# Moving padded chunk data as two transfers of 48 rows instead of one of 104, in a recurrence followed by two feed-forward layers

## The chip, the cores and the metric

The kernel runs on one core of a Trainium2 chip. The metric is the device time of one execution in microseconds (us), lower being better; the figure of a kernel is the median of its runs.

## The reference

Three stages follow one another. The first is a recurrence over 768 steps for 4 batches of 8 heads, each head with a state of 40 x 40; the second and third are feed-forward layers over the 3072 resulting tokens, with 320 inputs, 2048 hidden units and 320 outputs, all in float32.

```python
for t in range(S):                                # S = 768, state [B, H, 40, 40]
    y[:, :, t] = np.einsum('bhd,bhde->bhe', rt, state)
    Sa = np.einsum('bhde,bhe->bhd', state, at)
    state_decay = state * wt[:, :, None, :] - np.einsum('bhd,bhe->bhde', Sa, bt)
    state = state_decay + np.einsum('bhd,bhe->bhde', vt, kt)
...
h = x @ w_in;  g = h * (1.0 / (1.0 + np.exp(-1.702 * h)));  x = g @ w_out      # layer 1
h = x @ w_in;  g = h - np.tanh(h);                          x = g @ w_out      # layer 2
```

## The kernel before

The recurrence is cut into 24 chunks of 32 steps. For each chunk the products that do not need the state are formed first, then a small triangular system is inverted for a group of chunks, and then the state passes through the chunk.

The 32 heads (4 batches times 8) lie on the partitions as two halves, one at partitions 0 to 39 and one at 64 to 103, because each head has 40 channels and a half starts at a multiple of 64. The host pads each half to 64 rows, so one chunk is stored as 128 rows, of which rows 40 to 63 and 104 to 127 are padding. Moving rows 0 to 103 in one transfer takes both halves and the padding between them.

The methods that matter here:

- `early(c)` loads a chunk of `pin` into the buffer `P` (two buffers, used in turn). A row of `P` is 2065 floats: the decays at `OW`, then `a` at `OA`, then `k` and `b` from `OF` to `PC`. VectorE forms running products of the decays (L391, L397, L399), VectorE or GpSimd multiply them into the other parts (L394, L400, L402), TensorE forms the chunk's products (L416, L441). From chunk 2 on, the finished `P` is written to DRAM (`spill`), and small results go there too (`ka`, `ui`). `early` also loads `rve` (r and v) and `vns`.
- `inverse` and `inverse_halves` invert the triangular systems of a group of chunks, on GpSimd, step by step (L472, L475).
- `late(c)` brings the chunk's pieces back from `spill`, `ka` and `ui` in other layouts (`FW`, `L1`, `U`). `receptance(c)` loads `R`, and `decay(c)` reads `W` back from `spill`.
- `chain(c, g)` passes the state through chunk `c` (lines 608 to 683), and `store(c)` writes the result to DRAM.
- `layer1(j)` and `layer2(n)` are the two feed-forward layers (matrix products at L777). The seven blocks of `layer1` can start as soon as the chunks they need are stored, so they are interleaved with the recurrence.

All transfers are issued by SyncE through the helper `dma` (L367), so every issue has that line and is told apart by its tiles. SyncE takes them in the order in which they were put; an issue whose condition is not met holds up those behind it.

The order is static. Each `Plan.add` records a task with its engine, a planned cost, its reads and writes, and a rank. `Plan.run` then plays the tasks through a list scheduler (lowest rank first among those that are ready) and emits the instructions in that order, for each engine. A task with `alt` may be given to either of two engines. The ranks come from the constants at the top of the file (`ERANK`, `TRANK`, `L1RANK`, `LEAD`, `LATE` and others).

In the kernel before, a load of a chunk from chunk 2 on is one transfer:

```python
rows = 128 if c < 2 else 104
if c < 2:
    spans = [(OW, OA, [kw]), (OF, PC, kf), (OA, OF, [ka])]
else:
    spans = [(OW, PC, [kw, ka] + kf)]
```

Of the kernel before, what the change touches and what calls it, by code (L numbers as in the profile page):

```python
# [49 lines left out]
DENSE = 1.4  # L50
LEAD = 2.8824
OLAG = 1.5654
OLAG2 = 5.0633
PLAG = 1.9246
KLAG = -0.79715
W1RANK = -3.0783
W1STEP = 0.34953
W2RANK = 26.554
W2STEP = 0.79772
BUSY = -5  # L60
LATE = 2.3095
LATEK = 17.86
G1 = -0.86755
G2 = 0.47713
WI = 0.66347
WO = 0.31035
ERANK = [-10.488, -9.3866, -2.6101, -1.8742, -0.68695, 0.36407, 0.75062, 1.827, 2.2989, 3.1149, 4.0456, 5.1374, 6.4967,
         7.2956, 8.2655, 9.2836, 10.145, 11.291, 11.988, 12.804, 11.168, 15.748, 15.401, 16.869]
TRANK = [-10.117, 1.5844, 2.2273, 5.6823, 12.206, 5.8527, 13.273]
L1RANK = [2.1663, 6.6107, 7.7041, 11.297, 16.428, 24.217, 27.763]  # L70
L1STEP = [0.17239, 0.19469, 0.27164, 0.27454, 0.31295, 0.23795, 0.27849]
# [48 lines left out]

class Task:
# [3 lines left out]
class Plan:  # L125
# [6 lines left out]
    def add(self, eng, cost, fn, r=(), w=(), rank=0.0, bank=None, of=None, alt=None, size=0, after=(), warm=False):  # L132


        t = Task()
        t.eng, t.cost, t.fn, t.rank, t.bank, t.of, t.alt, t.size, t.warm = eng, cost, fn, rank, bank, of, alt, size, warm
        t.n, t.out, t.users, t.tile, t.started, t.soon = len(self.tasks), [], 0, None, False, 0.0
        deps = set(after)
        if of is not None:
            deps.add(of)  # L140
            of.users += 1

        t.after = {self.last[k] for k in (*r, *w) if k in self.last}
# [12 lines left out]
        t.left = len(deps)  # L156
        for d in deps:
            d.out.append(t)
        self.tasks.append(t)
        return t  # L160

    def run(self, free):
# [14 lines left out]
        while events and done < len(self.tasks):  # L177
# [19 lines left out]
            for e in free:  # L197
                while free[e] <= now:
# [42 lines left out]
                    if e == "pe":  # L241
# [7 lines left out]
                        work = t.cost * HEAT.get(t.cost, 0.76)  # L249
# [11 lines left out]
                    if e == "sp":  # L261

                        end, n = now, 2 if cost > 0.7 else 1
# [18 lines left out]
PHASE = 0  # L282
# [6 lines left out]
class Kernel:  # L289
    def __init__(self, ctx, tc, pin, rv, vn, cst, raw1, raw2, out):  # L290
# [7 lines left out]
        self.spill = dram.tile([NCH, 104, PC], F32, name="spill")  # L298
# [20 lines left out]
    def setup(self):  # L319
# [6 lines left out]
        nc.sync.dma_start(out=self.P[0][0:104, OW:OA], in_=self.pin[0, 0:104, OW:OA])  # L326
# [11 lines left out]
        self.W = two("W", 104, 16, 33)  # L338
# [29 lines left out]

    def early(self, c):
# [8 lines left out]
        rows = 128 if c < 2 else 104  # L378
        if c < 2:
            spans = [(OW, OA, [kw]), (OF, PC, kf), (OA, OF, [ka])]  # L380
        else:
            spans = [(OW, PC, [kw, ka] + kf)]
        for a, b, k in spans:
            if c or a != OW:
                add("sp", 0.475, lambda a=a, b=b: self.dma(wide[0:rows, a:b], self.pin[c, 0:rows, a:b]), w=k, rank=rank - 1.5, size=4 * rows * (b - a))
        w = P[:, OW:OW + 528]
        for i in range(2):
# [3 lines left out]
            add("dve", 0.345, lambda n=n, R=R: nc.vector.tensor_tensor_scan(  # L391
                out=R[:, ::-1], data0=P[:, OW + n + 1:OW + n + 265][:, ::-1], data1=self.d1[:, n + 1:n + 265][:, ::-1], initial=1.0,
                op0=ALU.mult, op1=ALU.add), r=[kw], w=[kr], rank=rank)
            add("pool", 1.19, lambda e, R=R, f=f: e.tensor_tensor(  # L394
                out=f, in0=f, in1=R.rearrange("p (o s t) -> p o s t", o=1, t=33)[..., 1:33].to_broadcast([104, 2, 8, 32]), op=ALU.mult),
                r=[kr], w=[kf[i]], rank=rank, alt=("dve", 0.6))
        add("dve", 0.6, lambda: nc.vector.tensor_tensor_scan(out=w, data0=w, data1=self.d1[:, 0:528], initial=1.0, op0=ALU.mult, op1=ALU.add),  # L397
            r=[kw], w=[kw], rank=rank)
        add("dve", 0.17, lambda: nc.vector.reciprocal(out=self.iwc[s], in_=W[:, :, 32:33]), r=[kw], w=[("iwc", s)], rank=rank)  # L399
        add("pool", 1.19, lambda e: e.tensor_tensor(out=W[:, :, 0:32], in0=W[:, :, 0:32], in1=self.iwc[s].to_broadcast([104, 16, 32]), op=ALU.mult),  # L400
            r=[("iwc", s)], w=[kw], rank=rank, alt=("dve", 0.6))
        add("pool", 1.19, lambda e: e.tensor_tensor(out=A, in0=A, in1=W[:, :, 0:32], op=ALU.mult), r=[kw], w=[ka], rank=rank,  # L402
            alt=("dve", 0.6))
        if c >= NEAR:
            add("sp", 0.475, lambda: self.dma(self.spill[c], P), r=[kw, ka] + kf, w=[("spill", c)], rank=rank + 1, size=858000)
# [13 lines left out]
        if c == 0 and GROUPS[0][1] < 4:  # L419
            m = GROUPS[0][1]  # L420
            add("pool", 0.5, lambda m=m: nc.gpsimd.memset(self.MA[:, m:], 0.0), w=[("MA", i) for i in range(m, 4)], rank=rank)
        krank = rank + (7.0 if c < NEAR else KLAG)
        t = add("pe", 1.5, mab, r=[ka] + kf, rank=rank + 0.2, bank="a" if c > AHEAD else "h")
        add("act", 0.27, lambda b: self.copy(self.MA[:, at], b.rearrange("p (Q t) -> p Q t", t=64)[:, :, 32:64]), w=[("MA", at)], rank=rank, of=t)
        add("dve", 0.34, lambda b: nc.vector.tensor_tensor(out=self.km, in0=b.rearrange("p (Q t) -> p Q t", t=64)[:, :, 0:32],
                                                           in1=self.maskt.unsqueeze(1).to_broadcast([128, 8, 32]), op=ALU.mult),
            w=["km"], rank=krank, of=t)
        add("dve", 0.34, lambda: nc.vector.transpose(out=self.kt[s], in_=self.km), r=["km"], w=[("kt", s)], rank=krank)
        if c >= NEAR:
            add("sp", 0.475, lambda: self.dma(self.ka[c], self.kt[s]), r=[("kt", s)], w=[("ka", c)], rank=krank + 1, size=131000)  # L430

        rank += 7.0 if c < NEAR else PLAG
        m = 128 if c == 0 else 104
        add("sp", 0.475, lambda: self.dma(self.rve[0:m].rearrange("p i s t -> p i (s t)"), self.rv[c, 0:m]), w=["rve"], rank=rank - 1.5, size=4096 * m)
        add("sp", 0.475, lambda: self.dma(self.vns, self.vn[c]), w=["vns"], rank=rank - 1.4, size=295000)
# [7 lines left out]
        t = add("pe", 1.1, prv, r=["rve"], rank=rank + 0.3, bank="a" if c > AHEAD else "h")  # L443
        add("dve", 0.34, lambda b: nc.vector.tensor_tensor(out=self.vns[:, :, 40:72], in0=b[:, 0:256].rearrange("p (Q t) -> p Q t", t=32),
                                                           in1=self.mask.unsqueeze(1).to_broadcast([128, 8, 32]), op=ALU.mult),
            w=["vns"], rank=rank, of=t)
        if c >= NEAR:
            add("sp", 0.475, lambda: self.dma(self.ui[c], self.vns), r=["vns"], w=[("ui", c)], rank=rank + 1, size=295000)

    def inverse(self, B, streams, rank):  # L450
# [3 lines left out]
        add("dve", 1.14, lambda: nc.vector.transpose(out=mu, in_=self.MA.rearrange("p c Q s -> p s (c Q)")),  # L454
# [8 lines left out]
        add("pool", 1.05, first, w=cols, rank=rank)  # L463
# [13 lines left out]
        for j in range(31):  # L477
            for name in ("dve", "pool"):
                now = [(k, eng[name], c0, min(c1, j + 1) - c0) for k, (e, c0, c1) in enumerate(streams) if e == name and j >= c0]
                if now:  # L480
# [3 lines left out]
                    add(name, cost, lambda j=j, now=now: step(j, now), r=["mu"], w=ks + [key for x in now for key in names[x[0]]], rank=rank)  # L484
        add("dve", 1.14, lambda: nc.vector.transpose(out=self.tt.rearrange("p u s -> p s u"), in_=tw), r=cols, w=[("tt", i) for i in range(4)], rank=rank)
# [7 lines left out]
    def inverse_halves(self, B, name, rank):  # L493
# [7 lines left out]
        add("dve", 1.14, lambda: nc.vector.transpose(out=mu, in_=self.MA.rearrange("p c Q s -> p s (c Q)")),  # L501
# [7 lines left out]
        add("pool", 1.05, first, w=cols, rank=rank)  # L509
# [13 lines left out]
        for j in range(15):  # L523
            els = 2 * (15 - j) * (j + 1)
            add(name, 0.4 + 1.65e-3 * els if name == "dve" else 0.5 + 3.74e-3 * els, lambda j=j: step(j), r=["mu"], w=cols + [("tmp", i) for i in range(4)], rank=rank)
        d, kd = (tt, [("tt", i) for i in range(4)]) if full else (mu, ["mu"])
        x0 = [("xf0", at, k) for at in (0, 64) for k in range(4)]
        add("dve", 1.14, lambda: nc.vector.transpose(out=d.rearrange("p u s -> p s u"), in_=tw), r=cols, w=kd, rank=rank)
        add("dve", 1.14, lambda: nc.vector.transpose(out=t2.rearrange("p u b -> p b u"), in_=tw.rearrange("p a b -> p b a")), r=cols, w=x0, rank=rank)
# [14 lines left out]
        for u in range(0, n, 8):  # L544
            c, o = (u0 + u) // 8, slice(u0 + u, u0 + u + 8)
            t = add("pe", 0.54, lambda b, u=u: p1(b, u), r=[("MA", c)] + kd, rank=rank, bank="a")
            add("act", 0.27, lambda b, u=u: self.copy(self.tmp[:, 16 * u:16 * u + 128], b[:, 0:128]), w=[("tmp", u // 8)], rank=rank, of=t)
            t = add("pe", 1.06, lambda b, u=u: p2(b, u), r=[("tmp", u // 8)] + x0, rank=rank, bank="a")
            if not full:
                add("dve", 0.2, lambda o=o: nc.vector.tensor_copy(out=tt[:, o, 0:16], in_=d[:, o, 0:16]), r=kd, w=[("tt", c)], rank=rank)  # L550
            add("dve", 0.2, lambda b, o=o: nc.vector.tensor_tensor(out=tt[:, o, 16:32], in0=b[:, 0:128].rearrange("p (u x) -> p u x", x=16),
                                                                  in1=d[:, o, 16:32], op=ALU.add), r=kd, w=[("tt", c)], rank=rank, of=t)

    def late(self, c):
# [10 lines left out]
        for h in range(2):  # L565
            for i in range(2):
                x = f[h][:, 0:4:3] if i == 0 else f[h][:, 1:3]
                q = 64 * (1 - h) + 32 * i
                add("sp", 2 * one, lambda x=x, q=q: (self.dma(self.FW[q:q + 32, 0], x[0:32]), self.dma(self.FW[q:q + 8, 1], x[32:40])),
                    r=kf, w=[("FW", h, i)], rank=rank, size=82000)  # L570

        for h in range(2):
            o = half(1 - h, 64)
            add("dve", 1.14, lambda h=h, o=o: nc.vector.transpose(out=self.LK[s][o, h].rearrange("p s (w e) -> p s w e", w=2),
                                                                 in_=self.FW[o].rearrange("p w x (Q t) -> p (x Q) w t", t=32)),
                r=[("FW", h, i) for i in range(2)], w=[("LK", s, h)], rank=rank + LATEK)
        for h in range(2):
            p = half(h)
            add("sp", one, lambda h=h, p=p: self.dma(self.L1[s][p, h], whole[p, OA:OF].rearrange("p (s t) -> p s t", s=16)),
                r=kl, w=[("L1", s, h)], rank=rank, size=82000)  # L580
        for j in range(4):
            q, a = quad(VQ[j]), slice(8 * (j % 2), 8 * (j % 2) + 8)
            add("sp", 2 * one, lambda j=j, q=q, a=a: (self.dma(self.L1[s][q, j // 2, a], ka[q]), self.dma(self.U[s][q, j // 2, a], ui[q])),
                r=kv, w=[("L1", s, 2 + j), ("Uv", s, j)], rank=rank, size=106000)

    def receptance(self, c):
        m = 128 if c == 0 else 104
# [426 lines left out]
```

## Time and profile before

| | |
|---|---|
| median of 3 runs | 1211.06 us (1210.31 to 1216.1) |
| profiled execution, own time | 1208.2 us |
| its span, first to last instruction | 1206.4 us |
| mean granted TensorE clock | 0.931 |
| TensorE busy | 1027.7 us (85%) |
| VectorE busy | 1006.3 us (83%) |
| ScalarE busy | 690.2 us (57%) |
| GpSimd busy | 528.1 us (44%) |
| moved by DMA | 145.84 MB |

The profiled execution lies 2.9 us below the median of the runs. Around the span there are 1.8 us that belong to the execution's own time. Busy shares are means over stages that differ: the recurrence and layer 1 fill the first 730 us together, the rest of layer 1 follows, and layer 2 is at the end.

### The profile page before, as it was taken

What the parts mean: (1) busy time and instruction counts of PE and PEld (TensorE: products, weight loads), DVE (VectorE), ACT (ScalarE), POOL (GpSimd) and SP (SyncE); (2) the same over time, 40 slices, a digit from 0 to 9 for tenths busy, and PEclk for the clock granted to TensorE, in tenths of its full rate; (3) what the DMA queues carried; (4) which work ended last, traced back from release to release, by engine and by line L of the source; (5) the groups of instructions that cost most, each with busy time, mean ns of one, the idle gap of its engine ahead of it and who ended that gap; (6) DMA issues with size and microseconds to landing.
All of it is one profiled execution on the core that took longest, in us unless ns stands there. A gap on an engine that the chain in (4) does not pass through costs nothing.

```text
span 1206.4 us, 36405 instructions
## 1 busy us (share of the span) xinstructions
PE 1027.7 (85%) x14862; PEld 861.8 (71%) x14862; DVE 1006.3 (83%) x1758; ACT 690.2 (57%) x1457; POOL 528.1 (44%) x647
## 2 busy tenths in 40 slices
PE   2354567787787999998799999999899999999998
PEld 1244456776775776676577777778698999899998
DVE  8778889988888767768786657999999998999896
ACT  4122244444453545443454556676888788888885
POOL 5638249857638611129548200112333333333332
PEclk9765679888899999899899999999999999999999
DMA  6868777766666455466444414242301010100000
GB/s 217 219 190 234 196 223 191 185 192 195 182 165 172 121 152 160 122 169 196 135 119 139 131 41 132 97 144 96 90 10 48 2 49 1 49 1 23 1 24 23
DMA packets 100391, 145.84 MB, mean 121 GB/s; under 512 B 35783, under 2 KB 70471, under 8 KB 95647
## 3 DMA queue, kind: packets, MB, share of 16 engines
q1 hardware_dynamic: 100223, 143.50, 42.1%
q8 instruction: 117, 1.92, 0.7%
q14 instruction: 51, 0.42, 0.1%
HBM read 101.11 MB, written 40.07 MB: 117 GB/s over the span
## 4 chain that ended last, share of the span: by engine, by line
PE 49%; DVE 18%; DMA 12%; POOL 8%; issue 6%; ACT 4%; SPq 3%; DVEq 0%; ACTq 0%; POOLq 0%
PE b L777 39%; DMA P<-in_pin_dram 5%; POOL tw L475 3%; POOL tmp L472 3%; SPq L367 3%; PE b L659 3%; PE b L683 2%; DVE gf L918 1%; PE b L635 1%; PE b L608 1%; DMA spill<-P 1%; PE b L624 1%; DVE wi L814 1%; DVE rp L391 1%; DMA rve<-in_rv_dram 1%
## 5 line engine op out<-in xcount | busy, mean ns | idle before, releaser
L795 POOL TENSOR_TENSOR gl<-gf,gh 128x512 fp32r<-128x512 f32 x95 | 123.4, 1299 | 208.1 <-ACT gh L364 194.4
L777 PE MATMUL b<-xh,wi 128*128 128x512 f32 (+1 forms) x672 | 200.6, 386 | 4.7 <-issue 2.7
L777 PE MATMUL b<-gh,wo 128*128 128x512 f32 (+1 forms) x560 | 189.9, 380 | 1.5 <-DVE wo L831 1.2
L824 POOL TENSOR_TENSOR gl<-gf,gh 128x512 fp32r<-128x512 f32 (+1 forms) x48 | 59.7, 1245 | 243.7 <-ACT gh L822 212.7
L777 PEld LDWEIGHTS b<-xh,wi 128*128 128x128 f32 x672 | 127.8, 202 | 31.5 <-issue 5.4
L777 PE MATMUL b<-gl,wo 128*128 128x512 f32 (+2 forms) x336 | 124.6, 374 | 14.1 <-DVE gl L824 9.5
L364 ACT ACTIVATE U<-b 32x160 f32<-32x160 f32 (+1 forms) x284 | 90.8, 321 | 77.3 <-PE b L608 31.6
L777 PEld LDWEIGHTS b<-gh,wo 128*128 128x128 f32 x560 | 107.2, 197 | 28.5 <-issue 2.6
L918 DVE SCALAR_TENSOR_TENSOR gf<-gs,guh 128x512 f32<-128x512 f32 x96 | 110.7, 1153 | 16.3 <-ACT gs L913 16.1
L472 POOL TENSOR_TENSOR tmp<-mu,tw 128x31 f32<-128x31 f32 (+15 forms) x155 | 101.3, 654 | 44.0 <-DVE mu L454 34.1
L364 ACT ACTIVATE wi<-T 128x384 fp32r<-128x384 f32 x112 | 58.3, 520 | 101.9 <-PE b L777 85.6
L475 POOL TENSOR_TENSOR tw<-tw,tmp 128x31 f32<-128x31 f32 (+15 forms) x155 | 105.8, 683 | 12.2
L777 PE MATMUL b<-xh,W 128*128 128x512 f32 x324 | 100.2, 392 | 2.2 <-DVE gf L920 2.2
L814 DVE TENSOR_TENSOR wi<-T,wi 128x384 fp32r<-128x384 f32 x112 | 79.0, 706 | 26.9 <-ACT wi L364 24.3
L364 ACT ACTIVATE wo<-T 128x320 fp32r<-128x320 f32 x112 | 52.2, 467 | 84.3 <-PE b L777 65.5
L777 PE MATMUL b<-W,gh 128*128 128x320 f32 x432 | 95.8, 309 | 0.8 <-DVE yo L941 0.8
L394 POOL TENSOR_TENSOR P<-P,rp 104x512 f32<-104x512 f32 x27 | 51.5, 1906 | 99.2 <-DVE rp L391 72.3
L364 ACT ACTIVATE gh<-gf 128x512 fp32r<-128x512 f32 x96 | 61.1, 636 | 51.4 <-DVE gf L920 50.7
L659 PE MATMUL b<-U,LK 128*40 128x72 f32 x1536 | 68.9, 243 | 24.4 <-DVE U L645 14.4
L777 PE MATMUL b<-xl,wi 128*128 128x512 f32 (+1 forms) x224 | 85.0, 379 | 4.4 <-DVE xl L769 4.4
L659 PEld LDWEIGHTS b<-U,LK 128*40 128x40 f32 x1536 | 57.7, 127 | 38.5 <-issue 17.8
L920 DVE COPY_PREDICATED gf<-gm,b 128x512 f32<-128x512 int32 x96 | 71.8, 748 | 9.5
(124 smaller groups left out, 2630.1 us busy)
## 6 DMA issues: line engine op xcount, KB each, us to landing
P<-in_pin_dram SPq DMA_DIRECT2D x22, 838.9 KB
spill<-P SPq DMA_DIRECT2D x22, 838.9 KB
xf<-in_raw_dram SPq DMA_DIRECT2D x16, 704.0 KB
raw<-in_raw_dram SPq DMA_DIRECT2D x16, 704.0 KB
rve<-in_rv_dram SPq DMA_DIRECT2D x23, 416.0 KB
vns<-in_vn_dram SPq DMA_DIRECT2D x24, 288.0 KB
ui<-vns SPq DMA_DIRECT2D x22, 288.0 KB
U<-ui SPq DMA_DIRECT2D x88, 72.0 KB
```

The costliest lines, as they stand in the source:

```text
L364: self.nc.scalar.activation(out=out, in_=in_, func=ACTF.Copy)
L367: self.nc.sync.dma_start(out=out, in_=in_)
L394: add("pool", 1.19, lambda e, R=R, f=f: e.tensor_tensor(out=f, in0=f, in1=R.rearrange("p (o s t) -> p o s t", o=1, t=33)[..., 1:33].to_bro ...
L472: e.tensor_tensor(out=o, in0=mu[:, j, j + 1:].unsqueeze(2).to_broadcast(sh), in1=tw[:, j:j + 1, c0:c0 + n].to_broadcast(sh), op=ALU.mult)
L475: e.tensor_tensor(out=t, in0=t, in1=o, op=ALU.subtract)
L659: nc.tensor.matmul(out=b[half(h), 72 * k:72 * k + 72], lhsT=LK[:, h, lo + k, 0:40], rhs=U[:, h, lo + k], start=True, stop=True)
L777: self.nc.tensor.matmul(out=out, lhsT=lhsT, rhs=rhs, start=start, stop=stop)
L795: add("pool", cost * 2.9, lambda e: e.tensor_tensor(out=gl(), in0=gf[:, c], in1=gh().bitcast(F32), op=ALU.subtract), r=[("gf", k % 2), ("g ...
L814: add("dve", 0.47, lambda hi=hi, lo=lo, T=T: nc.vector.tensor_tensor(out=lo, in0=T[:, 0:384], in1=hi.bitcast(F32), op=ALU.subtract), r=[(" ...
L824: add("pool", cost * 2.9, lambda e, gf=gf, gh=gh, gl=gl: e.tensor_tensor(out=gl[:, c], in0=gf[:, c], in1=gh[:, c].bitcast(F32), op=ALU.sub ...
L918: add("dve", 0.6, lambda g=g, gf=gf: nc.vector.scalar_tensor_tensor(out=gf, in0=g()[2], scalar=PK, in1=g()[4], op0=ALU.add, op1=ALU.mult), ...
L920: add("dve", 0.6, lambda b, g=g, gf=gf: nc.vector.copy_predicated(out=gf, mask=g()[3].bitcast(I32), data=b), r=[ke("m"), ke("d")], w=[("gf ...
```

## The change

From chunk 2 on, the load of a chunk becomes three transfers: one for the decays, over rows 0 to 111, and two for all the rest, over rows 0 to 47 and rows 64 to 111. The write to `spill` becomes two transfers of 48 rows, and so do the loads of `rve` and `R` (from chunk 1 on) and the reading of `W` back from `spill`. The reads of `L1` from `spill` take 48 rows where they took 40. The buffers `W` and `spill` grow from 104 to 112 rows. The planned cost of an issue that is now two doubles.

The constants of the order are all new. Besides, each `add` call now has a name, and a table `TUNE` gives each name a shift of its ranks and a factor on its planned cost; `OLAG` becomes a list with a value for each block of layer 1, and `PHASE`, the place of a grid in the scheduler's planned clock, changes from 0 to 2.54044. Instructions on the compute engines keep their number and shapes; which of two engines does a task with `alt`, and the order on each engine, can change.

```diff
-DENSE = 1.4
-LEAD = 2.8824
-OLAG = 1.5654
+DENSE = 1.12858
+LEAD = 4.13893
+OLAG = [0.321501828, 0.188656854, 0.496707663, 0.384020578, 0.494297397, 0.166910414, 0.338531745]
...
-LATE = 2.3095
-LATEK = 17.86
+LATE = 0.943511
+LATEK = 1.50372
...
-TRANK = [-10.117, 1.5844, 2.2273, 5.6823, 12.206, 5.8527, 13.273]
+TRANK = [-18.3004, 14.7221, 2.50279, 21.7466, 31.1652, 20.6657, 27.68]
...
+TUNE = {
+    "chain0": (1.36315, 0.996336), "chain1": (9.03583, 1.21576), "chain10": (-7.49377, 0.938608), "chain11": (3.0948, 2.4743),
...
+    "inverse0": (-3.66528, 0.954188), "inverse1": (32.3635, 2.61412), "inverse2": (6.71079, 1.00027), "inverse3": (-16.3949, 0.804252),
...
-    def add(self, eng, cost, fn, r=(), w=(), rank=0.0, bank=None, of=None, alt=None, size=0, after=(), warm=False):
+    def add(self, by, eng, cost, fn, r=(), w=(), rank=0.0, bank=None, of=None, alt=None, size=0, after=(), warm=False):
...
+        later, longer = TUNE.get(by, (0.0, 1.0))
+        t.work, t.many = cost * HEAT.get(cost, 0.76), 2 if cost > 0.7 else 1
+        rank, cost, alt = rank + later, cost * longer, alt and (alt[0], alt[1] * longer)
...
-        self.spill = dram.tile([NCH, 104, PC], F32, name="spill")
+        self.spill = dram.tile([NCH, 112, PC], F32, name="spill")
...
+    def both(self, out, in_):
+
+        for h in range(2):
+            self.dma(out[half(h, 48)], in_[half(h, 48)])
...
-        rows = 128 if c < 2 else 104
         if c < 2:
-            spans = [(OW, OA, [kw]), (OF, PC, kf), (OA, OF, [ka])]
+            spans = [(OW, OA, [kw], 128), (OF, PC, kf, 128), (OA, OF, [ka], 128)]
         else:
-            spans = [(OW, PC, [kw, ka] + kf)]
-        for a, b, k in spans:
+            spans = [(OW, OA, [kw], 112), (OA, PC, [ka] + kf, 96)]
+        for a, b, k, m in spans:
             if c or a != OW:
-                add("sp", 0.475, lambda a=a, b=b: self.dma(wide[0:rows, a:b], self.pin[c, 0:rows, a:b]), w=k, rank=rank - 1.5, size=4 * rows * (b - a))
+                f = (lambda a=a, b=b, m=m: self.dma(wide[0:m, a:b], self.pin[c, 0:m, a:b])) if m > 96 else (lambda a=a, b=b: self.both(wide[:, a:b], self.pin[c, :, a:b]))
+                add("early0", "sp", 0.475 if m > 96 else 0.95, f, w=k, rank=rank - 1.5, size=4 * m * (b - a))
...
-            add("sp", 0.475, lambda: self.dma(self.spill[c], P), r=[kw, ka] + kf, w=[("spill", c)], rank=rank + 1, size=858000)
+            add("early7", "sp", 0.95, lambda: self.both(self.spill[c], wide), r=[kw, ka] + kf, w=[("spill", c)], rank=rank + 1, size=793000)
...
-            p = half(h)
-            add("sp", one, lambda h=h, p=p: self.dma(self.L1[s][p, h], whole[p, OA:OF].rearrange("p (s t) -> p s t", s=16)),
-                r=kl, w=[("L1", s, h)], rank=rank, size=82000)
+            p = half(h, 48)
+            add("late2", "sp", one, lambda h=h, p=p: self.dma(self.L1[s][p, h], whole[p, OA:OF].rearrange("p (s t) -> p s t", s=16)),
+                r=kl, w=[("L1", s, h)], rank=rank, size=98000)
```

The loads of `rve` and `R` and the reading of `W` are changed to `both` in the same manner.

## Rows read from the trace of the kernel before

**Rows 1.** Busy time of each engine in seven stretches: granted clock, DMA share, GB/s.
```profile
core 0: us, PE busy (x) PEld busy (x) DVE busy (x) ACT busy (x) POOL busy (x), PEclk, DMA share, GB/s
0.00:180.00 180.00, 80.52 (x2489) 70.27 (x2489) 145.77 (x237) 55.20 (x114) 91.46 (x175) 0.72 0.75 214
180.00:420.00 240.00, 195.26 (x4443) 167.45 (x4444) 206.12 (x430) 111.81 (x303) 168.44 (x210) 0.91 0.64 176
420.00:510.00 90.00, 84.67 (x1551) 63.59 (x1551) 63.37 (x139) 45.30 (x108) 12.24 (x8) 0.96 0.54 147
510.00:600.00 90.00, 75.55 (x1188) 56.86 (x1188) 68.59 (x125) 37.79 (x85) 55.74 (x72) 0.92 0.62 167
600.00:730.00 130.00, 124.71 (x2760) 96.97 (x2761) 89.58 (x222) 68.97 (x177) 50.75 (x73) 0.99 0.36 101
730.00:930.00 200.00, 193.88 (x908) 158.54 (x908) 188.00 (x293) 151.69 (x283) 52.20 (x37) 1.00 0.30 91
930.00:1206.00 276.00, 273.07 (x1533) 248.16 (x1531) 244.83 (x319) 219.43 (x392) 97.29 (x75) 1.00 0.06 20
```

**Rows 2.** The chain that ended last, share of the span by engine.
```profile
PE 49%; DVE 18%; DMA 12%; POOL 8%; issue 6%; ACT 4%; SPq 3%; DVEq 0%; ACTq 0%; POOLq 0%
```

**Rows 3.** Pieces of that chain in order: start us, us, what.
```profile
47.34 8.16 DMA R<-in_rv_dram
55.52 12.70 DMA P<-in_pin_dram
...
75.87 6.37 DMA spill<-P
...
91.15 5.85 DMA xf<-in_raw_dram
...
115.13 8.64 DMA rve<-in_rv_dram
128.65 7.02 DMA P<-in_pin_dram
...
146.39 4.93 DMA xf<-in_raw_dram
...
266.29 9.51 DMA spill<-P
...
349.54 8.68 DMA P<-in_pin_dram
...
387.32 2.89 DMA R<-in_rv_dram
...
399.08 3.26 DMA W<-spill
...
469.92 7.06 DMA P<-in_pin_dram
...
498.79 6.74 DMA P<-in_pin_dram
...
531.89 7.80 DMA P<-in_pin_dram
...
638.80 5.34 DMA rve<-in_rv_dram
...
705.01 3.62 DMA W<-spill
```

**Rows 4.** Sizes of the transfers, each.
```profile
P<-in_pin_dram SPq DMA_DIRECT2D x22, 838.9 KB
...
xf<-in_raw_dram SPq DMA_DIRECT2D x16, 704.0 KB
...
W<-spill SPq DMA_DIRECT2D x22, 214.5 KB
```

**Rows 5.** Who waited for whom: us in total, times, longest.
```profile
DVE rp L391 <- DMA P<-in_pin_dram: 28.6, 11, 6.7
```

**Rows 6.** SyncE's issues of the chunk loads: ns min/median/max, first and last start us.
```profile
L367 SPq DMA_DIRECT2D P<-in_pin_dram x27: 312/345/1016, 1.6 to 584.5; - x27
```

More of the change, by code (lines that the diff above doesn't have):

```diff
@@ L248, in run @@
                         part = min(1.0, ((k + 1) * TICK - PHASE - now) / cost)
-                        work = t.cost * HEAT.get(t.cost, 0.76)
+                        work = t.work
                         heat[k] = heat.get(k, 0) + part * work
@@ L261, in run @@
                     if e == "sp":
-                        end, n = now, 2 if cost > 0.7 else 1
+                        end, n = now, t.many
                         for _ in range(n):
@@ L281 @@
 HOT = 1.0
-PHASE = 0
+PHASE = 2.54044
 X1 = [("xf1", k) for k in range(3)]
@@ L432, in early @@
         rank += 7.0 if c < NEAR else PLAG
[L433 to L435 removed]
+        m = 128 if c == 0 else 96
+        rve = self.rve.rearrange("p i s t -> p i (s t)")
+        add("early14", "sp", 0.475 if c == 0 else 0.95, (lambda: self.dma(rve, self.rv[0])) if c == 0 else (lambda: self.both(rve, self.rv[c])), w=["rve"],
+            rank=rank - 1.5, size=4096 * m)
@@ L437, in prv @@
+        add("early15", "sp", 0.475, lambda: self.dma(self.vns, self.vn[c]), w=["vns"], rank=rank - 1.4, size=295000)
         def prv(b):
@@ L461, in first @@
             nc.gpsimd.memset(tw.rearrange("p a b -> p (a b)")[:, 0::33], -1.0)
-        add("pool", 1.05, first, w=cols, rank=rank)
+        add("inverse1", "pool", 1.05, first, w=cols, rank=rank)
         bufs = (self.tmp, self.hs[0], self.km.rearrange("p a b -> p (a b)"))
@@ L483, in inverse @@
                     ks = [cols[x[0]] for x in now] if len(streams) > 1 else cols
-                    add(name, cost, lambda j=j, now=now: step(j, now), r=["mu"], w=ks + [key for x in now for key in names[x[0]]], rank=rank)
-        add("dve", 1.14, lambda: nc.vector.transpose(out=self.tt.rearrange("p u s -> p s u"), in_=tw), r=cols, w=[("tt", i) for i in range(4)], rank=rank)
+                    add("inverse2", name, cost, lambda j=j, now=now: step(j, now), r=["mu"], w=ks + [key for x in now for key in names[x[0]]], rank=rank)
+        add("inverse3", "dve", 1.14, lambda: nc.vector.transpose(out=self.tt.rearrange("p u s -> p s u"), in_=tw), r=cols, w=[("tt", i) for i in range(4)], rank=rank)
     def triangle(self, B):
@@ L507, in first @@
             nc.gpsimd.memset(tw.rearrange("p a b -> p (a b)")[:, 0::33], -1.0)
-        add("pool", 1.05, first, w=cols, rank=rank)
+        add("inverse_halves1", "pool", 1.05, first, w=cols, rank=rank)
         e = {"dve": nc.vector, "pool": nc.gpsimd}[name]
@@ L697, in f @@
                     self.dma(self.xs[0][40 * hd:40 * hd + 40, :, t0:t0 + 64], yt[half(hd % 4 // 2), hd % 2, :, hd // 4])
-            self.plan.add("sp", 1.3, f, r=[("yt", g, i, s) for g in range(2) for i in range(2) for s in range(2)], w=[("xs0", c // 2, n)],
+            self.plan.add("store0", "sp", 1.3, f, r=[("yt", g, i, s) for g in range(2) for i in range(2) for s in range(2)], w=[("xs0", c // 2, n)],
                           rank=c - LEAD, size=164000)
@@ L857, in layer1 @@
                 for q in ((0, 1, 2) if a else (2, 0, 1)):
-                    add("pe", mmt * (3 - q // 2) / 8, lambda q=q, outer=outer: outer(q), r=reads, w=[("acc", q)], rank=rank + step * OLAG, warm=True)
+                    add("layer17", "pe", mmt * (3 - q // 2) / 8, lambda q=q, outer=outer: outer(q), r=reads, w=[("acc", q)], rank=rank + OLAG[j], warm=True)
             else:
-                add("pe", mmt, outers, r=reads, w=[("acc", q) for q in range(3)], rank=rank + step * OLAG, warm=True)
+                add("layer18", "pe", mmt, outers, r=reads, w=[("acc", q) for q in range(3)], rank=rank + OLAG[j], warm=True)
@@ L891, in f @@
             self.acc = self.banks[5:8] + [self.banks[2]]
-        self.opened = self.plan.opener = self.plan.add("dve", 0.1, f, w=["cb"], after=ends, rank=-50)
+        self.opened = self.plan.opener = self.plan.add("open20", "dve", 0.1, f, w=["cb"], after=ends, rank=-50)
     def layer2(self, n):
```

212 lines of the change are left out of this document (109 added, 103 removed), and 23 rows, old and new, of the table TUNE.

## The prediction

> **What bounds the kernel now.** I read first the busy time by stretch, because shares over the whole span mix three different regimes [rows 1]. From 930 us to the end TensorE is busy 273.07 of 276.00 us at the full clock and the DMA share is 0.06: nothing that the change does to transfers reaches this stretch, and from 730 to 930 us TensorE is busy 193.88 of 200.00 us. From 0 to 180 us TensorE is busy only 80.52 of 180.00 us, at a granted clock of 0.72, while the DMA share is 0.75 and VectorE is busy 145.77 us. From 180 to 420 us it is idle for 44.74 us with the DMA share at 0.64. From 420 to 730 us (three rows) it is idle for 5.33, 14.45 and 5.29 us, 25.07 us in all. So time can be won almost only before 730 us, where TensorE stands idle for 99.48 + 44.74 + 25.07 = 169 us.
>
> Next I read the chain that ended last. By engine, DMA is 12% of it, about 145 us of 1206.4, and SyncE's queue 3%, about 36 us [rows 2]. In order of time the chain shows which transfers these are [rows 3]. Those that the change touches are six loads of `P` (12.70, 7.02, 8.68, 7.06, 6.74 and 7.80 us, 50.0 together), two writes of `spill` (15.9), two loads of `rve` (14.0), two of `R` (11.1) and three reads of `W` (first and last shown, 10.7 with the third of 3.80): 15 pieces, 101.7 us. The reader is to see that such a piece is time in which the whole kernel waits for that transfer, as far as the profile can tell. It is an upper limit, since another wait may end just after.
>
> **Part one: the transfers get shorter.** A load of `P` is 838.9 KB over 104 rows; a load of raw weights is 704.0 KB over 128 rows [rows 4]. The raw loads take 4.93 and 5.85 us on the chain, mean 5.39, so 131 KB per us; five of the `P` loads (without the first one of 12.70 us, which is far from the rest) take 7.46 us in the mean, so 112 KB per us [rows 3]. So 104 rows move more slowly per byte than 128. A row of `P` is 8260 bytes; afterwards the load is 112 rows of 2116 bytes and 96 of 6144, 807.4 KB, and the write of `spill` is 96 rows, 774.4 KB. If the new pieces move at the raw loads' mean rate, `P` takes 807.4 / 131 = 6.16 us instead of 7.46 (17% less) and `spill` 5.91 (21% less). On the chain that is 0.17 x 50.0 = 8.5 for `P` and 0.21 x (15.9 + 14.0) = 6.3 for `spill` and `rve`. `R` and `W` are small: a `W` of 214.5 KB takes 3.62 us, only 59 KB per us, so size is not most of their time. I give them half the rate, 0.105 x 21.8 = 2.3. Sum: 17 us. Low bound: only the bytes count, 3.8% of 50.0 and 7.7% of 51.7, 6 us. High bound: the best raw rate, 704.0 / 4.93 = 143 KB per us, which gives 24% of 50.0 and 27% of 51.7, 26 us. I take 17.
>
> The raw loads are distinguished by the number of rows, and the rows of the trace say no more than that. The Trainium skill, "DMA: Bandwidth & Descriptors", section "Why a DMA increments its semaphore by 16 and not by 1", gives a reason: a transfer is spread over the largest number of DMA engines, up to 16, that divides its count of rows, so 13 for 104 and 16 for 48, 112 and 128. By that, the busiest engine's load for `P` falls from 8 rows of 8260 bytes, 66.1 KB, to 7 of 2116 and 6 of 6144, 51.7 KB, 22% less instead of 17%, and the term would be about 22 us. The trace agrees in kind: by this rule `P` should take 66.1 / 45.1 = 1.47 times as long as a raw load, and 7.46 / 5.39 is 1.38.
>
> **Part two: the decays arrive ahead of the rest.** VectorE's scan L391 waits 28.6 us in 11 waits for `P` [rows 5], though it reads only the decays. Afterwards these have a transfer of their own of 231 KB, about the size of a `W`, which landed in 3.62 us [rows 3] where the whole `P` took 7.46. The scans can then run under the rest of the load. Most of this comes back as a wait at L394, which needs the other part, and VectorE has other work to go on with (145.77 of 180.00 us and 206.12 of 240.00 [rows 1]). Bounds: nothing, and the 28.6 us. I take 1 us for each of the six loads on the chain, 6 us.
>
> **Part three: more issues.** From chunk 2 on each chunk has two more issues for `P` and one more each for `spill`, `rve`, `R` and `W`: 6 x 22 = 132, and 2 for chunk 1, so 134. At the median of 345 ns [rows 6] that is 46 us more on SyncE's queue, where the reads of `FW`, `L1` and `U` for the next chunk, and `store`'s writes, stand behind them. What hides them: the first half is moving for some microseconds while the second is issued, and the queue runs ahead of its users. Without that cover, 46 us. The chain is now in this queue for 36 of 730 us, about 5%, and 5% of 46 is 2.3; since the issues stand in the crowded part I take twice that, 5 us. Eight more rows in each `L1` read add 16 KB to 80, 44 times: 0.12 us each by the raw rate, none of it on the chain in rows 3; I cost it at nothing, covered by the `FW` reads issued just ahead of it, and at 5 us if that cover is gone.
>
> **Part four: the order.** The compute instructions stay; where they stand changes on every engine. No row of before shows the new order. The gain is bounded by idle that an order could fill: the 25.07 us of TensorE between 420 and 730 us, where GpSimd is idle for 78 of the first 90 us and then busy for 55.74 of 90 us on the next inverse, while TensorE idles 14.45 us [rows 1]. An earlier inverse would take that away. The loss is bounded by the same row from the other side: the new ranks put the inverse's steps behind more of GpSimd's other work (`TRANK` and `TUNE` raise them), and a second group arriving as late costs another 14.45 us, two of them 29. Nearest to neither, I take 0 and keep -25 and +29.
>
> **Sum**, against the profiled execution's own 1208.2 us: -17 - 6 + 5 + 0 = -18, so 1190.2. The median of the runs is 2.9 us above that execution, so on its scale 1193. I say 1192. What can be told from no change is 0.5%, 6 us.
>
> **The rivals.**
>
> *The order gains as well* (1167 us, chance 0.22). The same 18 us, and the 25 us of TensorE's idle between 420 and 730 us. For it: GpSimd's idle ahead of the inverse. Against it: an inverse can't start before its four chunks are loaded, and the last three loads of the chain stand at 469.92, 498.79 and 531.89 us.
>
> *Hidden anyway* (1206 to 1214 us, chance 0.16). The shorter transfers uncover VectorE, which is idle only 34 us in each of the first two stretches. For it: VectorE at 81% and 86%. Against it: on the chain the transfers stand one by one, with VectorE's work after them, not beside them.
>
> *SyncE's queue takes over* (1234 us, chance 0.11). All 46 us of new issues are exposed: 1211 - 23 + 46. It decides from the point at which half of them, 23 us, cost time. For it: the queue is already 3% of the chain. Against it: 12% is transfers.
>
> *The halves move one after the other* (1221 us, chance 0.05). Each pair pays a second fixed part. From the two sizes, 7.46 us for 838.9 KB and 3.62 for 214.5, that part is about 2.3 us; fifteen of them are 34 us, and with the other terms -17 - 6 - 1 + 34 = +10 on 1211. Against it: `W`, `R` and `P` of one chunk are issued while earlier ones are still in flight, so fixed parts overlap. This is a rule of the Trainium skill, "DMA: Bandwidth & Descriptors", section "Rules for kernel authors", which speaks against this change: two transfers to disjoint halves of the partitions serialize and should be one of 128 rows. The trace has no such pair.
>
> **How the numbers follow.** The forecast, 1177 to 1204 us, has a chance of 0.46. Faster by over 0.5% is it and the first rival, 0.68; within 0.5% is the second, 0.16; slower are the last two, 0.16. The range is from the first rival's 1167, with 1 us more, to 1219: below are the best orders with the high bound of part one, above most of the queue's rival, about 1 in 10 each.
>
> **What would show it.** Right: the loads of `P` on the chain at about 6 us and their sum below 45; the scan's wait for `P` near half of 28.6 us; the DMA share of the first 180 us below 0.75 or TensorE's busy time there above 80.52 us; 730 us to the end unchanged in length, with the point where only layer 2 is left some 18 us earlier. Wrong: pieces of SyncE's queue on the chain well above 36 us; a longer wait of GpSimd or TensorE at the group boundaries; or the transfers shorter and VectorE's pieces of the chain longer by as much.

## The result, and the profile after

The changed kernel takes 1191.66 us in the median of 4 runs (1188.34 to 1193.5), beside 1211.34 us for the kernel before; the ratio is 0.983, with a 95% interval of 0.9802 to 0.9858. The forecast was 1192 us. The experiments show that this time came about in another way than the one forecast, so the profile after has to be read with care. Two of the 12 executions of one experiment, decays_last, ran at a lower granted clock (0.825 and 0.564) and took 1247.54 and 1635.69 us; its figures below leave them out.

The busy time by stretch, with the columns of [rows 1] (the last stretch ends with the shorter span):

```profile
0.00:180.00 180.00, 82.32 (x2705) 72.22 (x2706) 147.55 (x246) 55.74 (x116) 101.03 (x185) 0.84 0.77 208
180.00:420.00 240.00, 201.01 (x4430) 169.66 (x4430) 207.50 (x434) 116.92 (x311) 157.77 (x196) 0.93 0.69 179
420.00:510.00 90.00, 80.28 (x1523) 60.62 (x1523) 67.72 (x150) 41.07 (x103) 12.23 (x10) 0.94 0.60 151
510.00:600.00 90.00, 79.08 (x1316) 60.96 (x1316) 68.47 (x124) 39.63 (x91) 57.70 (x73) 0.94 0.61 159
600.00:730.00 130.00, 126.72 (x2531) 99.33 (x2532) 92.28 (x222) 74.52 (x186) 43.19 (x68) 1.00 0.38 106
730.00:930.00 200.00, 192.56 (x915) 158.39 (x914) 185.94 (x279) 152.86 (x281) 70.37 (x47) 1.00 0.26 79
930.00:1191.00 261.00, 258.21 (x1452) 234.88 (x1450) 198.93 (x304) 206.86 (x373) 93.91 (x72) 1.00 0.06 20
```

Against [rows 1], TensorE does 2705 matmuls in the first 180 us where it did 2489, at a mean granted clock of 0.84 instead of 0.72, and it is busy 5.75 us longer from 180 to 420 us. The DMA share did not fall: 0.77 instead of 0.75, and 0.69 instead of 0.64. The first line of the DMA queue's part of the page says the same of the whole span (packets, MB, share of 16 engines), first for the kernel before, then for the changed one:

```profile
q1 hardware_dynamic: 100223, 143.50, 42.1%
```
```profile
q1 hardware_dynamic: 104976, 140.68, 43.6%
```

Fewer bytes keep the 16 engines busy for longer: 0.421 x 1206.4 = 508 us before, 0.436 x 1191.7 = 520 us after. I call this product the engines' time.

The chain that ended last, by engine, answers to [rows 2]:

```profile
PE 51%; DVE 16%; DMA 11%; POOL 8%; issue 6%; SPq 4%; ACT 3%; DVEq 0%; POOLq 0%; ACTq 0%
```

The loads of `P` and of `rve` on that chain, in order of time, answer to those of [rows 3] (as there, the load of the first chunk, at 1.65 us, is left out):

```profile
103.24 5.63 DMA P<-in_pin_dram
...
127.41 5.79 DMA P<-in_pin_dram
...
185.12 4.44 DMA P<-in_pin_dram
...
257.30 6.32 DMA P<-in_pin_dram
...
273.07 4.60 DMA P<-in_pin_dram
...
289.81 4.33 DMA P<-in_pin_dram
...
316.70 4.26 DMA rve<-in_rv_dram
...
329.52 5.47 DMA rve<-in_rv_dram
...
342.49 4.41 DMA P<-in_pin_dram
...
417.81 4.94 DMA P<-in_pin_dram
...
437.11 4.04 DMA P<-in_pin_dram
...
475.77 5.11 DMA P<-in_pin_dram
...
520.96 4.93 DMA P<-in_pin_dram
```

Each piece of `P` is shorter than any before, 4.0 to 6.3 us against 6.7 to 12.7; a piece is now one of the three transfers of a load. But there are eleven where there were six, and together they take 54.5 us where they took 50.0. A reader who looks only at the length of a piece sees a success; the sum says that the chain waits for the loads of `P` as long as ever. The other transfers that the change touches did leave the chain: `spill`, `R` and `W` have no piece on it any more, and `rve` has 9.7 us where it had 14.0. All five together have 64.3 us where they had 101.7. That is not the gain either, as order_alone shows below.

The waits for `P`, answering to [rows 5] (us in total, times, longest):

```profile
DVE P L433 <- DMA P<-in_pin_dram: 22.0, 8, 6.0
...
POOL P L433 <- DMA P<-in_pin_dram: 19.3, 3, 9.5
...
DVE rp L430 <- DMA P<-in_pin_dram: 7.5, 5, 2.8
```

The scan (L430, formerly L391) waits 7.5 us instead of 28.6. The multiplication behind it (L433, formerly L394), which needs the rest of `P`, now waits 22.0 us on VectorE and 19.3 on GpSimd, where in the kernel before it waited once, for 2.3 us.

### The profile page after: what moved, and what is told of

Read it like the earlier page. It is cut to its first block, busy times and chain, and to the rows that moved or that the text cites. A ratio compares the mean times of both kernels' runs of the same rounds, so it can differ in the third digit from the quotient of the medians.

```text
span 1191.7 us, 36467 instructions
## 1 busy us (share of the span) xinstructions
PE 1020.2 (86%) x14862; PEld 856.1 (72%) x14862; DVE 968.4 (81%) x1755; ACT 687.6 (58%) x1457; POOL 536.2 (45%) x650
## 4 chain that ended last, share of the span: by engine, by line
PE 51%; DVE 16%; DMA 11%; POOL 8%; issue 6%; SPq 4%; ACT 3%; DVEq 0%; POOLq 0%; ACTq 0%
PE b L822 43%; DMA P<-in_pin_dram 5%; SPq L401 4%; POOL tw L516 2%; POOL tmp L513 2%; DMA xf<-in_raw_dram 2%; PE b L704 2%; PE b L680 2%; PE b L669 1%; PE b L653 1%; DVE U L709 1%; DMA FW<-spill 1%; POOL tw L562 1%; DVE P L436 1%; PE b L728 1%
## 5 line engine op out<-in xcount | busy, mean ns | idle before, releaser
L840 POOL TENSOR_TENSOR gl<-gf,gh 128x512 fp32r<-128x512 f32 x91 | 119.9, 1317 | 206.4 <-ACT gh L398 206.4
L822 PE MATMUL b<-xh,wi 128*128 128x512 f32 (+1 forms) x672 | 196.7, 384 | 4.8 <-ACT gh L867 3.1
L822 PE MATMUL b<-gh,wo 128*128 128x512 f32 (+1 forms) x560 | 185.7, 375 | 1.8 <-DVE wo L876 0.7
L869 POOL TENSOR_TENSOR gl<-gf,gh 128x512 fp32r<-128x512 f32 (+1 forms) x46 | 64.2, 1396 | 209.3 <-ACT gh L867 196.8
L867 ACT ACTIVATE gf<-b 128x512 f32<-128x512 f32 (+1 forms) x112 | 59.9, 535 | 103.1 <-PE b L822 98.1
L961 DVE TENSOR_TENSOR guh<-b,gu 128x512 f32<-128x512 f32 x96 | 65.9, 690 | 51.6 <-ACT gu L956 47.9
L433 POOL TENSOR_TENSOR P<-P,rp 104x512 f32<-104x512 f32 x30 | 49.5, 1651 | 115.9 <-DVE rp L430 31.4
L859 DVE TENSOR_TENSOR wi<-T,wi 128x384 fp32r<-128x384 f32 x112 | 82.9, 743 | 6.2 <-ACT wi L398 6.0
L957 ACT ACTIVATE gt<-b 128x512 f32<-128x512 f32 x96 | 57.5, 599 | 47.8 <-PE b L822 47.3
L822 PE MATMUL b<-xh,V 128*128 128x512 f32 x252 | 78.5, 393 | 3.2 <-DVE gf L965 3.2
L690 DVE TENSOR_TENSOR U<-b,cs 32x128 f32<-32x128 f32 x192 | 55.1, 287 | 28.1 <-PE b L680 20.8
```

The source lines that it names most:

```text
L690: nc.vector.tensor_tensor(out=u[..., 40:72], in0=x[..., 40:72], in1=self.mask[o].unsqueeze(1).to_broadcast([32, 4, 32]), op=ALU.mult)
L822: self.nc.tensor.matmul(out=out, lhsT=lhsT, rhs=rhs, start=start, stop=stop)
L840: add("split_g1", "pool", cost * 2.9, lambda e: e.tensor_tensor(out=gl(), in0=gf[:, c], in1=gh().bitcast(F32), op=ALU.subtract), r=[("gf", ...
L859: add("layer11", "dve", 0.47, lambda hi=hi, lo=lo, T=T: nc.vector.tensor_tensor(out=lo, in0=T[:, 0:384], in1=hi.bitcast(F32), op=ALU.subtr ...
L867: add("layer13", "act", 0.055 + cost, lambda b, o=o: nc.scalar.activation(out=o[:, c], in_=b[:, c], func=ACTF.Gelu_apprx_sigmoid), w=[key] ...
L869: add("layer14", "pool", cost * 2.9, lambda e, gf=gf, gh=gh, gl=gl: e.tensor_tensor(out=gl[:, c], in0=gf[:, c], in1=gh[:, c].bitcast(F32), ...
```

## The experiments

Theory M, that of the forecast: the transfers are shorter, and this brings the time; the order is neutral. Rival O: the new order brings it. All ratios are to the kernel before, timed in turn with it on the same chip; the experiments ran on three chips, so the ratios are to be compared, not the medians.

| run | order | transfers | median, us | ratio (95%) |
|---|---|---|---|---|
| the change | after | two of 48 | 1191.66 | 0.983 (0.9802 to 0.9858) |
| moves_alone | before | two of 48 | 1206.37 | 0.9943 (0.9923 to 0.9963) |
| order_alone | after | one of 104 | 1191.96 | 0.9829 (0.9797 to 0.986) |
| one_of_112 | before | one of 112 | 1195.03 | 0.9841 (0.9807 to 0.9875) |
| two_of_40 | before | two of 40 | 1191.89 | 0.9826 (0.9791 to 0.9861) |
| decays_last | before | two of 48, decays behind | 1208.57 | 0.9957 (0.9927 to 0.9987) |
| after_40 | after | two of 40 | 1178.19 | 0.9734 (0.9703 to 0.9765) |
| after_112 | after | one of 112 | 1174.07 | 0.9692 (0.9659 to 0.9725) |
| twice_112 | after | 112 rows, cut in two by columns | 1173.73 | 0.9664 (0.9633 to 0.9696) |
| after_128 | after | one of 128 | 1171.28 | 0.964 (0.9605 to 0.9675) |
| rv_whole | after | as after; `rve`, `R` one of 112 | 1187.20 | 0.9776 (0.9743 to 0.9808) |
| other_order | another | two of 48 | 1249.82 | 1.0311 (1.0279 to 1.0343) |

**moves_alone**: the order of before on all compute engines, with the new transfers put in the places of the old ones. The lines are shortened to the calls, and the comment is not in the kernel; `rve`, `R` and `W` use `both` in the same way, and `L1` is read with 48 rows.

```diff
-lambda a=a, b=b: self.dma(wide[0:rows, a:b], self.pin[c, 0:rows, a:b])
+lambda a=a, b=b: self.load_P(wide, c, a, b)      # decays of 112 rows, then two halves of 48
...
-lambda: self.dma(self.spill[c], P)
+lambda: self.both(self.spill[c], wide)
```

> The order of before, unchanged on all compute engines, with the transfers of after put in the same places. Theory M (the shorter transfers bring the time): 17 + 6 us less and some 5 us more for issues, so about 1193 us, ratio 0.985. Rival O (the new order brings it, and the old order can't use shorter transfers): within 5 us of before, 1206 to 1216 us. Rival Q (SyncE's queue pays for the issues, and the new order hides that): above 1216 us.

Measured: 0.9943, so 0.57%, 7 us (by the interval 4 to 9 us). Theory M asked for 0.985, 18 us, and is refuted; the rival's 5 us lie within the interval. The transfers bring something in the old order, a quarter to a half of what was forecast.

**order_alone**: the order of after on all compute engines, with transfers of 104 rows.

```diff
     def both(self, out, in_):
-        for h in range(2):
-            self.dma(out[half(h, 48)], in_[half(h, 48)])
+        if True:
+            self.dma(out[0:104], in_[0:104])
...
-            p = half(h, 48)
+            p = half(h)
```

The load of the decays takes 104 rows too, from chunk 2 on. It stays a transfer of its own ahead of the rest, so this part of the change is still in the run.

> The order of after, unchanged on all compute engines, with transfers of 104 rows in place of the pairs, 40 rows in the reads of L1, and the decays still loaded ahead of the rest. Theory M: the 17 us for shorter transfers come back, less the 5 us for issues saved: about 1204 us, ratio to before 0.994. Rival O: as after, 1192 us. If the new order is fitted to the new transfers, the old ones are late at every place where it counts on them: above 1211 us.

Measured: 0.9829, as after (0.983). In the new order the pairs of 48 are worth nothing against one transfer of 104. Rival O's number is met, theory M's is not. The profiled run shows it as well: its last recurrence matmul on `R` starts at 699.3 us (min/median/max ns, first and last start us), where that of the changed kernel starts at 704.7 us, in the second fence:

```profile
L653 PE MATMUL b<-R,SN x1472: 191/199/274, 87.1 to 699.3; 64*40 64x32 f32 x184
```
```profile
L653 PE MATMUL b<-R,SN x1472: 186/199/273, 86.6 to 704.7; 64*40 64x32 f32 x184
```

In the kernel before this was:

```profile
L608 PE MATMUL b<-R,SN x1472: 191/199/272, 80.9 to 718.6; 64*40 64x32 f32 x184
```

Two more readings of this run bear on the argument. Its first two stretches, with the columns of [rows 1]:

```profile
0.00:180.00 180.00, 78.67 (x2628) 68.63 (x2631) 143.76 (x237) 52.79 (x107) 95.89 (x179) 0.66 0.73 208
180.00:420.00 240.00, 205.12 (x4543) 173.28 (x4530) 216.41 (x447) 121.13 (x322) 163.26 (x202) 0.94 0.69 192
```

The granted clock of the first 180 us is 0.66, below the 0.72 of the kernel before and the 0.84 of the changed one, and the time is that of the changed kernel. So the higher clock there is not what brings the gain. From 180 to 420 us TensorE is busy 9.9 us longer and VectorE 10.3 us longer than in [rows 1].

The pieces of `spill` and `W` on its chain are:

```profile
88.01 9.32 DMA spill<-P
...
231.38 4.92 DMA W<-spill
...
263.01 9.73 DMA spill<-P
...
469.98 9.16 DMA W<-spill
...
493.05 7.44 DMA W<-spill
...
544.47 10.32 DMA spill<-P
```

With seven loads of `P` (42.1 us), one of `R` (7.0) and one of `rve` (7.5), the touched transfers have 107.5 us of this chain. The changed kernel has 64.3 us of them on its own and is no faster. So a microsecond less of these pieces on the chain is not a microsecond less of the kernel.

**one_of_112**: the order of before, `rows = 128 if c < 2 else 112`, and 112 for 104 in `spill`, `rve`, `R` and `W`, with the planned sizes left as they were.

> The order of before, with one transfer of 112 rows wherever 104 were moved: 7.7% more bytes and not one issue more. If a transfer is shared out by a divisor of its row count (13 for 104, 16 for 112), the busiest share falls from 8 rows to 7: loads of P about 10% shorter, some 8 us less, 1203 us, ratio 0.993. If only the bytes count: 7.7% longer on about 100 us of the chain, 1215 us or more, ratio 1.004 to 1.006.

Measured: 0.9841, a gain of 1.59% with 7.7% more bytes in these transfers. So fewer bytes are not what helps; it gains twice what was expected for the better sharing.

**two_of_40**: as moves_alone, with 40 rows in each half and in `L1`.

```diff
-        self.dma(out[half(h, 48)], in_[half(h, 48)])
+        self.dma(out[half(h, 40)], in_[half(h, 40)])
```

> The order of before, with the pairs at 40 rows each instead of 48 (the decays of P still 112 rows ahead, L1 as before): the fewest bytes. If bytes and the early decays bring the gain: at least as fast as the pairs of 48, below 1193 us. If a divisor of the row count shares the work out (10 for 40, so 4 rows in each of two transfers, 8 on the busiest, as with 104): only the early decays gain, 1200 to 1208 us, slower than the pairs of 48.

Measured: 0.9826, a gain of 1.74%, three times that of the pairs of 48. The number is that of the first guess, but with one_of_112 beside it that guess can't be the cause: more bytes in 112 rows gain as much as fewer bytes in two of 40, as far as the intervals tell. Of the new shapes the odd one out is 48. (`L1` has 48 rows in moves_alone and 40 here; no run in the old order changes that alone.)

**by_itself**: only transfers, one after another has landed (the second half of a pair doesn't wait for the first). It computes nothing of the reference and fills the output with zeros.

```diff
+for name, rows in (("m128", [(0, 128)]), ("m112", [(0, 112)]), ("m104", [(0, 104)]),
+                   ("m48", [(0, 48), (64, 112)]), ("m40", [(0, 40), (64, 104)])):
+    ...
+    for c in range(8):
+        for a, b in rows: self.dma(t[a:b], self.pin[c, a:b])
+    for c in range(8):
+        for a, b in rows: self.dma(d[a:b], t[a:b])
```

> The transfers alone: nothing of the reference is computed (the output is filled with zeros). Eight loads of a whole chunk of pin into one buffer and eight writes to DRAM, each after the one before it has landed, for five shapes: one transfer of 128, 112 or 104 rows, two of 48, two of 40. Theory E (the work of a transfer is shared by a divisor of its row count; each sharer has its own rate): 8, 7, 8, 6 and 8 rows on the busiest, so 48 is the shortest, 25% under 104, and 40 is as long as 104. Theory S (a limit that the sharers have in common, which rows of one half reach sooner): a pair is no faster than 104 rows in one, although it moves fewer bytes.

Measured, by stretch: eight loads, then eight writes, for 128, 112, 104, 48 + 48 and 40 + 40 rows in this order; the last three columns are the clock, the DMA share and GB/s:

```profile
13.00:51.90 38.90, 0.00 (x0) 0.00 (x0) 1.00 0.65 226
51.90:81.80 29.90, 0.00 (x0) 0.00 (x0) 1.00 0.60 248
81.90:130.50 48.60, 0.00 (x0) 0.00 (x0) 1.00 0.61 174
130.50:163.70 33.20, 0.00 (x0) 0.00 (x0) 1.00 0.60 195
163.80:218.70 54.90, 0.00 (x0) 0.00 (x0) 1.00 0.58 142
218.70:259.60 40.90, 0.00 (x0) 0.00 (x0) 1.00 0.54 147
259.60:300.60 41.00, 0.00 (x0) 0.00 (x0) 1.00 0.82 174
300.60:330.40 29.80, 0.00 (x0) 0.00 (x0) 1.00 0.85 199
330.40:366.30 35.90, 0.00 (x0) 0.00 (x0) 1.00 0.58 156
366.30:398.00 31.70, 0.00 (x0) 0.00 (x0) 1.00 0.48 171
```

The first load of a shape is issued while the last write of the shape ahead of it is still on its way, so these stretches are not quite clean. From the issue of the second load to that of the first write there are seven loads, and nothing of another shape:

```profile
18.19:51.90 33.71, 0.00 (x0) 0.00 (x0) 1.00 0.63 220
89.94:130.54 40.60, 0.00 (x0) 0.00 (x0) 1.00 0.57 160
173.60:218.75 45.15, 0.00 (x0) 0.00 (x0) 1.00 0.56 133
268.06:300.66 32.60, 0.00 (x0) 0.00 (x0) 1.00 0.84 169
335.84:366.38 30.54, 0.00 (x0) 0.00 (x0) 1.00 0.56 150
```

Both theories fall. A pair of 48 loads in 32.60 / 7 = 4.7 us where 104 rows take 6.5, so it is faster alone, against S. But 128 and 104 rows should be equal by E and are 4.8 and 6.5 us, and 40 + 40 should be as long as 104 and is 4.4; 112 rows take 5.8. The Trainium skill's divisor ("DMA: Bandwidth & Descriptors", section "Why a DMA increments its semaphore by 16 and not by 1"), which I had weighed in part one, does not give these times by itself. What the first table shows besides is the share: the pairs of 48 keep the engines 0.82 and 0.85 busy. Share times length, loads and writes together, is about 43.2 us for 128 rows, 49.6 for 112, 53.9 for 104, 59.0 for two of 48 and 36.0 for two of 40. Divided by 128, 112, 104, 96 and 80 rows, this is 0.34, 0.44, 0.52, 0.61 and 0.45 us of an engine for one row of the same 8260 bytes (16 engines share 16 transfers, so the two numbers cancel). So theory E fails in its second half: a row does not cost an engine the same in every shape. And a pair of 48 is quick while nothing else moves, but takes more of the engines than 104 rows in one.

**after_40** and **after_112**: the order of after, with `half(h, 40)` in `both`, or with `self.dma(out[0:112], in_[0:112])` in place of its loop; `L1` of 40 rows.

> The order of after with pairs of 40 rows, and 40 rows in the reads of L1. If fewer bytes help wherever they are moved, as they did in the order of before: below after, 1180 to 1188 us. If the new order has no more use for shorter transfers, as its being as fast with 104 rows says: 1192 us, within 4 us.

> The order of after with one transfer of 112 rows in place of each pair, and 40 rows in the reads of L1. If the new order is indifferent to the shape: 1192 us, within 4 us. If 112 rows help as they did in the order of before: 1180 to 1188 us.

Measured: 0.9734 and 0.9692. The new order is not indifferent to transfers; of the shapes tried it is only the pair of 48 that is no better than 104. Against order_alone, 112 rows gain 1 - 0.9692 / 0.9829 = 1.4%, about the 1.59% that they gain in the old order: for this shape, order and transfers add up. In the profiled run of after_112 the recurrence's last matmul on `R` comes 20.8 us before that of the changed kernel:

```profile
L653 PE MATMUL b<-R,SN x1472: 186/199/273, 84.5 to 683.9; 64*40 64x32 f32 x184
```

**twice_112**: `both` issues columns up to the middle, then the others, for 112 rows.

> The order of after with 112 rows in place of 48 and 48, but each such transfer cut in two by columns, so that there are as many issues as with the pairs; 40 rows in the reads of L1. If the issues are what the pairs of 48 cost: about 1190 us, as after. If it is the rows that a transfer takes: about 1176 us, as with 112 rows in one.

Measured: 0.9664, not slower than after_112 (0.9692, the intervals overlap). The additional issues cost nothing that can be measured in this order.

**rv_whole**: as after, but `rve` and `R` of 112 rows in one, `L1` of 40 rows.

> As after, but rve and R come in one transfer of 112 rows, and L1 takes 40 rows; P, spill and W keep their pairs of 48. If the large pairs (P and spill) cost the time that 112 rows save: 1186 to 1192 us, near after. If the small pairs and the 48 rows of L1 cost it: 1174 to 1180 us.

Measured: 0.9776, so 0.5% under after (the intervals just touch), of 1.4% between after and after_112. Most of the difference lies with the pairs that this kernel keeps, `P`, `spill` and `W`. The 0.5% also bounds what the 48 rows of `L1` cost in the new order, since they are among what was changed.

**decays_last**: as moves_alone, with the two lines of `load_P` exchanged.

> As moves_alone (the order of before, the transfers of after), but the decays of a chunk are issued behind the two halves instead of ahead of them. If their coming early is worth the 6 us of the forecast: 1212 us. If it is worth nothing: 1206 us, within 2 us.

Measured: 0.9957, beside 0.9943; the intervals overlap widely. That the decays come first can't be told from nothing, and the forecast's 6 us (0.5%) lie at the edge of what the two intervals allow.

**after_128**: one transfer of 128 rows for each pair and for the decays.

> The order of after with one transfer of 128 rows in place of each pair and for the decays; 40 rows in the reads of L1. 14% more bytes than 112 rows. By itself a load of 128 rows took 38.9 us for eight where 112 rows took 48.6 and pairs of 48 took 41.0. If the time for which a transfer keeps the DMA engines busy decides (0.65 x 38.9 = 25 for 128 rows, 0.61 x 48.6 = 30 for 112, 0.82 x 41.0 = 34 for pairs of 48, and 0.60 x 29.9 = 18, 20 and 25 for the writes): 1165 to 1174 us. If the bytes decide: above 1176 us.

Measured: 0.964, 3.6% below the kernel before, though it moves 13.4 MB more than it (156.88 against 143.50). It is the lowest ratio of all, but the intervals of twice_112 and after_112 overlap with its own.

**other_order**: all of after, with one planned size changed, which no transfer depends on.

```diff
-size=4 * m * (b - a)
+size=4 * (104 if m == 112 else m) * (b - a)
```

> The transfers and the constants of after; only the planned size of the load of the decays is that of 104 rows instead of 112. That alone changes the order on every engine from the first 200 us on. If the constants as such make the order good (earlier inverses, other ranks): 1188 to 1198 us. If the good order is one that these constants hit only with exactly these planned sizes: well above 1200 us, perhaps as before.

Measured: 1.0311, so 4.9% above after with the same constants and the same transfers. So the order is that sensitive to a planned size. Its recurrence ends late:

```profile
L653 PE MATMUL b<-R,SN x1472: 186/199/273, 87.3 to 772.1; 64*40 64x32 f32 x184
```

## Why the prediction was right, and where its steps were wrong

The time and the sign were right, and so was the place: from the last matmul on `R` to the end it is 487.8 us before (1206.4 - 718.6) and 487.0 us after (1191.7 - 704.7), so nearly all of the gain lies ahead of it. The terms were not right, and that they added up to the measured time is luck.

**Part one, "the transfers get shorter", 17 us**: the pieces of `P` did get shorter, by more than forecast (mean of the eleven 4.96 us, forecast 6.16, though one piece is now one transfer of three). The step that failed is to take what a piece loses on the chain off the time of the kernel: in the new order the pairs bring 0 (order_alone against after), in the old one 7 us together with part two. The text called the chain's 101.7 us an upper limit and then priced 17 us of it as if no other wait ended just behind. The runs speak for such waits: 107.5 and 64.3 us of these pieces on the chain go with the same time (order_alone and after). What the pairs of 48 cost in exchange is in part shown: more of the engines' time, 59.0 against 53.9 us by itself, 518 against 508 in the old order (moves_alone, 0.428 x 1209.2, against before) and 520 against 507 in the new one (after against order_alone). That other transfers are held up by this, and that it eats the gain, is a reading that fits; no run changed it alone.

**Part two, the early decays, 6 us**: the scan's wait fell further than forecast, to 7.5 us where half of 28.6 was expected. What became of it depends on the order. The idle time, ahead of instructions on `P`, that a load of `P` ended (us in total, times), in the kernel before, moves_alone, order_alone and the changed kernel:

```profile
  DMA P<-in_pin_dram: 30.9, 12
```
```profile
  DMA P<-in_pin_dram: 15.2, 9
```
```profile
  DMA P<-in_pin_dram: 41.2, 15
```
```profile
  DMA P<-in_pin_dram: 48.9, 16
```

In the old order the new transfers halve this wait, so most of what the scan saves does not come back at the multiplication; still the kernel gains only 4 to 9 us. In the new order the wait is long with either transfers, so the long waits at L433 come with the order. The place of the decays alone is worth less than can be told (decays_last, in the old order).

**Part three, the issues, 5 us**: nothing that can be measured in the new order (twice_112), although the chain's share of SyncE's queue rose from 3% to 4%, 36 to 48 us. By the text that was a sign of being wrong; a larger share of the chain was no cost here. The rival built on it, 1234 us, falls with it.

**Part four, the order, 0 us, kept at -25 and +29**: this is the term that carried the result. It was worth 1 - 0.9829 = 1.71% of 1211.51, 20.7 us (order_alone, which has the decays as a transfer of their own in it). The bound held, the value taken did not. The forecast met the time because an order worth 21 us replaced transfers worth 18. The bound on the other side was too near: other_order, the same constants with one planned size changed, lies 3.1% above the kernel before, 38 us, and 4.9% above after, 58 us.

Of the other signs that the text gives, two came true without deciding anything. The pieces of `P` are short, but their sum is above 45 us. TensorE's busy time in the first 180 us is above 80.52 us, but the DMA share is not below 0.75, and order_alone reaches the same time with 78.67.

The rival *the order gains as well* had half of it right: the order gains, but for 48 rows the transfers then add nothing; with 112 rows they do add, and its 1167 us is nearly reached by after_128. The rival *the halves move one after the other* is not borne out: by itself a pair of 48 loads in 4.7 us where 104 rows take 6.5. Its sum has a slip: it takes -1 us where part three is +5, and with +5 it would have been 1227 us. Nor is it so that the trace of the kernel before has no pair of halves: the reads of `L1` are such pairs, of 40 rows each, though nothing in that trace compares them with one transfer.

What stays open: why 104 rows in one are so slow by themselves (133 GB/s beside 220 for 128 rows); and why two of 40, which use the engines least, are behind 128 rows in the new order (0.9734 and 0.964). The engines' time alone doesn't rank the shapes: the whole kernel after_112 keeps the engines busy as long as order_alone within 2 us (0.432 x 1171.1 = 506 and 0.427 x 1188.3 = 507) and is 1.4%, 17 us, faster. Which part of the new order gains the 21 us was not tried.

## What to carry to other kernels

A transfer's piece on the chain is at most a bound on what shortening it can give, and no price for it: here 43 us less of such pieces gave nothing. Look at a transfer's length by itself and at its share of the DMA engines times that length; neither alone ranked the shapes here. Before padding is cut away, try one transfer of all 128 rows: in this kernel no shape was faster, and it moved the most bytes. When a change comes with a new static order, run the new order with the old moves and the old order with the new moves before giving the gain to either.

## What the hardware showed that I had not expected

By itself, a load of 128 rows of 8260 bytes took 4.8 us, of 112 rows 5.8 and of 104 rows 6.5: fewer rows, longer. Two transfers of 48 rows kept the DMA engines 0.84 busy at 169 GB/s, where 112 rows in one moved at 160 GB/s with a share of 0.57.
